# Attention steps joined for two units, six weight conversions moved from stage one to the slots, one Square moved from ScalarE to VectorE

## The chip, the cores and the metric

The kernel runs on one core of a Trainium2 chip. The metric is the time of one execution in microseconds (us), as the device measures it; lower is better. Beside it stands a profile of one execution, whose "span" runs from its first to its last recorded instruction. The engines are called PE (TensorE, the matrix unit), DVE (VectorE), ACT (ScalarE), POOL (GpSimd) and SP (SyncE, which here issues most of the DMAs, in the order in which they stand in its queue).

## The reference

```
def _attn_ref(q, k, v, g_norm):
    kv = np.einsum('bhsd,bhse->bhde', k, v)
    out = np.einsum('bhsd,bhde->bhse', q, kv)
    rms = np.sqrt(np.mean(out * out, axis=-1, keepdims=True) + 1e-06)
    return (out / rms * g_norm).astype(np.float32)
def _moe_ref(x, w_in, w_out):
    h = x @ w_in
    r = np.maximum(h, 0.0)
    g = r * r
    return (g @ w_out).astype(np.float32)
def _moe2_ref(x, w_in, w_out):
    h = x @ w_in
    g = h * np.cos(h)
    return (g @ w_out).astype(np.float32)
```

There are 8 batches of 8 heads, 576 positions and a head width of 64. The attention's output becomes a matrix x of 4608 tokens by 512, which goes through `_moe_ref` (512 to 2048 to 512) and then through `_moe2_ref` with other weights of the same shape. The weights come in float64 words, two 32-bit halves each.

## The kernel before

Every factor of a matmul that has to be exact is kept as a high and a low part (`xh` and `xl`, `wh` and `wl`, `gh` and `gl`), and a product is three matmuls: high by high, high by low, low by high. The name "conversion" below means the work on one piece of weights: a load of raw words into a buffer `raw`, then on DVE `e` (L119), `w` (L121, L124), `e` (L130), the value (L133) and sums of blocks (L177), on ACT a step on `e` (L120) between the first two and the high part `wh` (L189), on DVE the low part (L191), and then stores of both to DRAM (L193, L194), from which the matmuls' loads `wi` and `ws` fetch them later. The pool of `raw` has two buffers. The load of the conversion after next is issued (L148) once the stores of the earlier one in that buffer are through. `Stream.place` gives each conversion its position and cuts it into steps at small distances after that position.

**Stage one** is 72 chunks, counted by `n`: 9 tiles of 512 tokens by 8 blocks `f` of 128 columns of the first layer. A chunk is 12 matmuls of the first layer into one PSUM bank (`layer_in`, L385), the activation `act_relu2` (Relu, L394; Square, L395; high part `gh`, L396; all on ACT; low part `gl` on DVE, L397), and 12 matmuls of the second layer into four accumulators (`layer_out`, L419), two chunks later. In chunks up to `nAtt` = 49 the attention runs in between, in units: a pair of heads `p` of a batch `b`, by two halves `i`. Its banks are "o" and "ss"; from chunk 49 on all four banks `l0`, `l1`, `o`, `ss` serve the first layer. A unit goes through `att_a` (PE), `att_o` (ACT: `sq` L305, `og` L306, and for batches from `NEXACT` = 2 on also `sh` L312, then `sl` on DVE L313), `att_b` (PE sums of squares `ss`, ACT `r` L325 and `r2` L327), `att_c` (DVE, L335 to L337) and `att_e` (stores to DRAM, `x_d`). In the first two batches, called the head below, `att_d` also writes some pieces directly into `xh` and `xl`.

**The slots** follow: 30 of them, 10 for the first MoE's remaining blocks and 20 for the second MoE. In a slot seven products of blocks go into the banks FA and FB (`first_product`, L507), are combined on DVE and ACT (`h`, L531), and go through a second set of products into SA and SB (L606, L669). The loads `wi` (L481) for the products stand in SP's queue among the conversions' loads and stores.

Positions in the list `jobs` order the calls; a scheduler that knows the buffers then fixes the order on each engine. The list of conversions is placed by

```
        (pairs_in(0, range(NP, 2 * NP)) + pairs_in(1, range(3)), nAtt + 1, nA0 - 7),
        (pairs_in(1, range(3, 2 * NP)) + pairs_in(1, range(4, 6), "seven"), pos(1), pos(7)),
```

that is 14 conversions spread over chunks 50 to 65 and 14 over slots 1 to 7. `nA0` = 72 is the number of chunks and `pos(k)` the start of slot k.

Of the kernel before, what the change touches and what calls it, by code (L numbers as in the profile page):

```python
# [16 lines left out]
P = 128  # L17
# [5 lines left out]
def kernel(  # L23
# [278 lines left out]
    def att_o(o, *u):  # L302
        og = att_p.tile([P, HS], F32, tag="og", name="og", bufs=4)
        sq = att_p.tile([P, HS], F32, tag="sq", name="sq", bufs=3)
        nc.scalar.activation(out=sq, in_=o, func=AF.Square)  # L305
        nc.scalar.activation(out=og, in_=o, func=AF.Copy, scale=gcol)  # L306
        if u[0] < NEXACT:
            att[u] = (og, sq, None)
            return
        sh = att_p.tile([P, HS], F32R, tag="sh", name="sh", bufs=2)  # L310
        sl = att_p.tile([P, HS], F32R, tag="sl", name="sl", bufs=2)
        nc.scalar.copy(out=sh, in_=sq)  # L312
        nc.vector.tensor_tensor(out=sl, in0=sq, in1=as32(sh[:]), op=ALU.subtract)  # L313
        att[u] = (og, sh, sl)

    def att_b(*u):
        og, sh, sl = att[u]
        ss = bank("ss")[:, :HS]
        if u[0] < NEXACT:
            nc.tensor.matmul(ss, as32(ones[:]), sh[:], start=True, stop=True)  # L320
        else:
            nc.tensor.matmul(ss, ones[:], sh[:], start=True, stop=False)
            nc.tensor.matmul(ss, ones[:], sl[:], start=False, stop=True)
        r = att_p.tile([P, HS], F32, tag="r", name="r", bufs=2)
        nc.scalar.activation(out=r, in_=ss, func=AF.Abs_reciprocal_sqrt, scale=1.0 / D, bias=epsb)  # L325
        r2 = att_p.tile([P, HS], F32, tag="r2", name="r2", bufs=2)
        nc.scalar.activation(out=r2, in_=r, func=AF.Square)  # L327
        att[u] = (og, ss, r, r2)

    def att_c(*u):  # L330

        og, ss, r, r2 = att[u]
        m = att_p.tile([P, HS], F32, tag="m", name="m", bufs=2)
        xo = att_p.tile([P, HS], F32, tag="xo", name="xo", bufs=3)
        nc.vector.scalar_tensor_tensor(out=m, in0=ss, scalar=D * EPS, in1=r2, op0=ALU.add, op1=ALU.mult)  # L335
        nc.vector.scalar_tensor_tensor(out=m, in0=m, scalar=-3.0 * D, in1=r, op0=ALU.add, op1=ALU.mult)
        nc.vector.tensor_tensor(out=xo, in0=m, in1=og, op=ALU.mult)  # L337
        att[u] = xo

    def att_d(*u):  # L340
        b, p, hf = u
        xo = att[u]
        if b >= NEXACT:
# [622 lines left out]
```

## Time and profile before

| what | value |
|---|---|
| runs | 1589.66, 1588.98, 1587.4 us (median 1588.98) |
| the profiled execution's own time | 1588.0 us |
| its span | 1586.2 us |
| PE busy | 1552.5 us (98%) |
| DVE busy | 1243.9 us (78%) |
| ACT busy | 1073.7 us (68%) |
| HBM traffic over the span | 246 GB/s |

The time is some 1.8 us longer than the span. PE's busy time counts a matmul from its start to its modelled end, so two that follow each other overlap; whether PE runs at its pace in a stretch is seen better from the number of matmuls that start in it than from the busy share. [...]

### The profile page before, as it was taken

The page shows a single profiled execution, that of the slowest core. Times are in us where ns is not written, and L with a number is a line of the kernel's source. Part 1 is how long each engine was busy: PE and PEld are TensorE (multiplying, and loading weights), DVE is VectorE, ACT ScalarE, POOL GpSimd, SP SyncE. Part 2 cuts the span into 40 slices and gives each one's busy share as a digit, 9 for nine tenths or more (in the row PEclk, how much of TensorE's full clock was granted, in tenths as well). Part 3 has the DMA queues.
Part 4 walks back from the last instruction along what each step waited for, and adds up shares of the span by engine and source line. Part 5 has one row for each costly group of instructions (what it writes and reads, how often), then busy time and mean ns, then how long its engine had stood idle before and what let it go on. Part 6 is the DMA issues. An engine that isn't in the chain of part 4 may idle for free.

```text
span 1586.2 us, 24792 instructions
## 1 busy us (share of the span) xinstructions
PE 1552.5 (98%) x9164; PEld 1359.8 (86%) x9164; DVE 1243.9 (78%) x1688; ACT 1073.7 (68%) x1535; POOL 116.4 (7%) x125
## 2 busy tenths in 40 slices
PE   5999999999989999999999999999999999999998
PEld 4777777778777878888999899999999999999998
DVE  7977868798766798888747678967896788689677
ACT  5977768775545755555636667776777677777774
POOL 1100211111100000000000000000000001100110
PEclk9999999999999999999999999999999999999999
DMA  8855978777679989999987678988999889999995
GB/s 320 276 157 163 279 225 248 217 212 225 213 221 333 320 263 340 312 345 304 339 273 288 231 215 270 269 260 262 268 264 280 239 259 287 279 365 308 265 363 170
DMA packets 236951, 425.53 MB, mean 268 GB/s; under 512 B 18464, under 2 KB 155168, under 8 KB 236832
## 3 DMA queue, kind: packets, MB, share of 16 engines
q1 hardware_dynamic: 225840, 387.78, 72.9%
q0 software_dynamic: 10992, 36.18, 11.3%
q8 instruction: 73, 1.20, 0.3%
q14 instruction: 46, 0.38, 0.1%
HBM read 309.85 MB, written 80.22 MB: 246 GB/s over the span
## 4 chain that ended last, share of the span: by engine, by line
PE 83%; DVE 6%; DMA 5%; issue 3%; ACT 2%; SPq 0%; POOL 0%; DVEq 0%; ACTq 0%; POOLq 0%
PE FA L507 15%; PE FB L507 15%; PE SA L669 13%; PE SB L669 12%; PE acc L419 9%; PE l L385 9%; PE SB L606 3%; PE SA L606 3%; DMA wi_d<-raw 1%; DMA raw<-in_wB 1%; DMA sum<-part 1%; DMA q<-in_qT 1%; DVE raw L177 1%; ACT wh L189 1%; DMA raw<-in_wA 1%
## 5 line engine op out<-in xcount | busy, mean ns | idle before, releaser
L507 PE MATMUL FA<-xh,wi 128*128 128x512 f32 (+1 forms) x840 | 306.1, 370 | 1.1 <-ACT ev L405 0.9
L507 PE MATMUL FB<-xh,wi 128*128 128x512 f32 (+1 forms) x840 | 306.1, 370 | 0.0
L669 PE MATMUL SB<-ws,gh 128*128 128x256 f32 x1008 | 237.9, 280 | 1.1 <-ACT u L521 0.8
L669 PE MATMUL SA<-ws,gh 128*128 128x256 f32 x1008 | 237.9, 280 | 0.0
L669 PEld LDWEIGHTS SB<-ws,gh 128*128 128x128 f32 x1008 | 185.9, 188 | 14.4 <-ACT u L521 1.0
L669 PEld LDWEIGHTS SA<-ws,gh 128*128 128x128 f32 x1008 | 186.2, 188 | 13.2
L507 PEld LDWEIGHTS FA<-xh,wi 128*128 128x128 f32 x840 | 157.8, 188 | 11.0 <-ACT ev L405 1.3
L507 PEld LDWEIGHTS FB<-xh,wi 128*128 128x128 f32 x840 | 157.8, 188 | 8.2
L646 DVE TENSOR_TENSOR gl<-y,gh 128x1024 fp32r<-128x1024 f32 (+1 forms) x100 | 111.4, 1114 | 39.1 <-ACT gh L645 38.9
L669 PE MATMUL SA<-ws,gl 128*128 128x256 f32 x504 | 141.0, 280 | 1.1 <-DVE gl L646 1.1
L669 PE MATMUL SB<-ws,gl 128*128 128x256 f32 x504 | 141.2, 280 | 0.8 <-DVE gl L646 0.8
L695 POOL DMA_DIRECT2D sum<-part x71 | 60.3, 850 | 1100.8 <-ACT part L694 1082.2
L566 DVE SCALAR_TENSOR_TENSOR y<-y,h 128x1024 f32<-128x1024 f32 (+1 forms) x80 | 89.2, 1115 | 53.6 <-ACT y L562 53.2
L548 ACT ACTIVATE y<-h,zerob 128x1024 int32<-128x1024 f32 (+1 forms) x80 | 85.1, 1064 | 50.7 <-DVE h L527 50.7
L419 PE MATMUL acc<-gh,wh 128*128 128x512 f32 x288 | 114.5, 399 | 4.2 <-ACT gh L396 2.5
L419 PE MATMUL acc<-gl,wh 128*128 128x512 f32 x288 | 114.4, 397 | 2.1 <-DVE gl L397 2.1
L419 PE MATMUL acc<-gh,wl 128*128 128x512 f32 x288 | 113.6, 395 | 0.0
L507 PE MATMUL FA<-xl,wi 128*128 128x512 f32 (+1 forms) x300 | 111.0, 370 | 0.0
L507 PE MATMUL FB<-xl,wi 128*128 128x512 f32 (+1 forms) x300 | 110.9, 370 | 0.0
L669 PEld LDWEIGHTS SB<-ws,gl 128*128 128x128 f32 x504 | 94.7, 188 | 7.9 <-DVE gl L646 1.5
L669 PEld LDWEIGHTS SA<-ws,gl 128*128 128x128 f32 x504 | 94.7, 188 | 7.8 <-DVE gl L646 1.3
L645 ACT CAST gh<-y 128x1024 fp32r<-128x1024 f32 (+1 forms) x100 | 94.5, 957 | 6.1 <-DVE y L628 6.0
(178 smaller groups left out, 3781.6 us busy)
## 6 DMA issues: line engine op xcount, KB each, us to landing
wi<-wi_d SPq DMA_DIRECT2D x210, 512.0 KB, 6.9
ws<-ws_d SPq DMA_DIRECT2D x175, 512.0 KB, 5.8
sum<-part POOLq DMA_DIRECT2D x45, 512.0 KB, 7.7
kvld<-in_kv SPq DMA_DIRECT2D x32, 512.0 KB, 6.9
wi_d<-wh SPq DMA_DIRECT2D x24, 448.0 KB, 4.1
wi_d<-raw SPq DMA_DIRECT2D x24, 448.0 KB, 4.0
raw<-in_wA SPq DMA_DIRECT2D x20, 512.0 KB, 5.5
wo<-wo_d SPq DMA_DIRECT2D x20, 512.0 KB, 6.4
```

The source lines that it names most:

```text
L177: nc.vector.tensor_tensor(out=a[:, o], in0=a[:, x], in1=a[:, y], op=op)
L189: nc.scalar.copy(out=h, in_=a[:, lo:end])
L385: nc.tensor.matmul(ps, a[:, 0, cs], m[:], start=(c == 0 and k == 0), stop=(c == NKC - 1 and k == 2))
L419: nc.tensor.matmul(o, a[:, cs], m[:], start=(f == 0 and n == 0), stop=(f == NH - 1 and n == 2), skip_group_check=True)
L507: nc.tensor.matmul(ps[:, pp, :], a, b, start=(i in (0, 1, 2) and n == 0), stop=(n == 5), skip_group_check=True)
L548: nc.scalar.activation(out=y.bitcast(I32), in_=hs[k, b], func=AF.Identity, bias=zerob)
L566: nc.vector.scalar_tensor_tensor(out=y, in0=y, scalar=-2.0 * math.pi, in1=hs.pop((k, b)), op0=ALU.add, op1=ALU.mult)
L606: nc.tensor.matmul(ps, lhs, rhs, start=(a == 0 and (x, y) == (0, 0)), stop=last, skip_group_check=True)
L645: nc.scalar.copy(out=h, in_=src)
L646: nc.vector.tensor_tensor(out=l, in0=src, in1=as32(h), op=ALU.subtract)
L669: nc.tensor.matmul(ps[:, b, :], lhs, rhs, start=(i in (0, 1, 2) and n == 0 and (m == 0 or b % 2 == 0)), stop=(n == 5), skip_group_check=True,)
L695: nc.gpsimd.dma_start(out=e, in_=part, accum_op=ALU.add)
```

## The change

It has four parts. The attention's operations that touch SBUF alone (`sh`, `sl`, the second step of `att_c` and its product) are done once for the two units of a pair, on tiles of [128, 2, 288] in place of two of [128, 288]; the result takes the place of `m`, whose three buffers `sq` of the later batches shares; `r` and `r2` have one buffer in place of two; `x_d` is stored once both units are done. In the 23 chunks from 49 on, Square on ACT is replaced by one DVE operation that reads the PSUM bank and `r`. The steps of a conversion in the chunks after `nAtt` are spaced as before it. Six conversions (`pairs_in(1, range(3))`) move to the slots: 8 are spread over chunks 50 to 65, and 20 over slots 1 to 9.2.

```diff
@@ -299,52 +299,57 @@
         for i, o in enumerate(os):
             att_o(o, b, p, i)
 
-    def att_o(o, *u):
-        og = att_p.tile([P, HS], F32, tag="og", name="og", bufs=4)
-        sq = att_p.tile([P, HS], F32, tag="sq", name="sq", bufs=3)
-        nc.scalar.activation(out=sq, in_=o, func=AF.Square)
-        nc.scalar.activation(out=og, in_=o, func=AF.Copy, scale=gcol)
-        if u[0] < NEXACT:
-            att[u] = (og, sq, None)
+    def two(dtype, name, tag, bufs):
+        return att_p.tile([P, 2, HS], dtype, tag=tag, name=name, bufs=bufs)
+
+    def att_o(o, b, p, i):
+        if i == 0:
+            sq = two(F32, "sq", "sq", 2) if b < NEXACT else two(F32, "sq", "m", 3)
+            att[b, p] = {"og": two(F32, "og", "og", 2), "sq": sq}
+        a = att[b, p]
+        nc.scalar.activation(out=a["sq"][:, i], in_=o, func=AF.Square)
+        nc.scalar.activation(out=a["og"][:, i], in_=o, func=AF.Copy, scale=gcol)
+        if b >= NEXACT and i == 1:
+            sq = a["sq"]
+            a["sh"], a["sl"] = sh, sl = two(F32R, "sh", "sq", 2), two(F32R, "sl", "sl", 2)
+            nc.scalar.copy(out=sh, in_=sq)
+            nc.vector.tensor_tensor(out=sl, in0=sq, in1=as32(sh[:]), op=ALU.subtract)
+
+    def att_b(b, p, i):
+        a = att[b, p]
+        ss = a["ss", i] = bank("ss")[:, :HS]
+        if b < NEXACT:
+            nc.tensor.matmul(ss, as32(ones[:]), a["sq"][:, i], start=True, stop=True)
+        else:
+            nc.tensor.matmul(ss, ones[:], a["sh"][:, i], start=True, stop=False)
+            nc.tensor.matmul(ss, ones[:], a["sl"][:, i], start=False, stop=True)
+        if i == 0:
+            a["r"] = two(F32, "r", "r", 1)
+        r = a["r"][:, i]
+        nc.scalar.activation(out=r, in_=ss, func=AF.Abs_reciprocal_sqrt, scale=1.0 / D, bias=epsb)
+        r2 = a["r2", i] = att_p.tile([P, HS], F32, tag="r2", name="r2", bufs=1)
+        nc.scalar.activation(out=r2, in_=r, func=AF.Square)
+
+    def att_c(b, p, i):
+
+        a = att[b, p]
+        if i == 0:
+            a["m"] = two(F32, "m", "m", 3)
+        m = a["m"]
+        nc.vector.scalar_tensor_tensor(
+            out=m[:, i], in0=a["ss", i], scalar=D * EPS, in1=a["r2", i], op0=ALU.add, op1=ALU.mult
+        )
+        if i == 1:
+            nc.vector.scalar_tensor_tensor(out=m, in0=m, scalar=-3.0 * D, in1=a["r"], op0=ALU.add, op1=ALU.mult)
+            nc.vector.tensor_tensor(out=m, in0=m, in1=a["og"], op=ALU.mult)
+
+    def att_d(b, p, i):
+        if b >= NEXACT or i == 0:
             return
...
-    def att_d(*u):
-        b, p, hf = u
-        xo = att[u]
-        if b >= NEXACT:
-            return
-        tok = b * S + hf * HS
+        xo = att[b, p]["m"].rearrange("p i n -> p (i n)")
+        tok = b * S
         for t in range(NDIRECT):
-            lo, hi = max(tok, t * TOK), min(tok + HS, (t + 1) * TOK)
+            lo, hi = max(tok, t * TOK), min(tok + S, (t + 1) * TOK)
             if lo >= hi:
                 continue
             if (t, p) not in xs:
@@ -354,16 +359,18 @@
             nc.scalar.copy(out=h, in_=piece)
             nc.vector.tensor_tensor(out=l, in0=piece, in1=as32(h), op=ALU.subtract)
 
-    def att_e(*u):
-        b, p, i = u
-        xo = att.pop(u)
-        if b < NEXACT:
-            nc.gpsimd.dma_start(out=x_d[b][:, p, i * HS:(i + 1) * HS], in_=xo)
+    def att_e(b, p, i):
+        if i == 0:
             return
-        for hf in range(2):
-            nc.sync.dma_start(
-                out=x_d[b][i * D:(i + 1) * D, p, hf * HS:(hf + 1) * HS], in_=xo[hf * D:(hf + 1) * D]
-            )
+        xo = att.pop((b, p))["m"]
+        for i in range(2):
+            if b < NEXACT:
+                nc.gpsimd.dma_start(out=x_d[b][:, p, i * HS:(i + 1) * HS], in_=xo[:, i])
+                continue
+            for hf in range(2):
+                nc.sync.dma_start(
+                    out=x_d[b][i * D:(i + 1) * D, p, hf * HS:(hf + 1) * HS], in_=xo[hf * D:(hf + 1) * D, i]
+                )
 
     def att_units(b):
         return [(b, p, i) for p in range(NKC) for i in range(2)]
@@ -387,12 +394,15 @@
                     )
         return pss
 
-    def act_relu2(ps):
+    def act_relu2(ps, busy):
         r, g = (temp([P, TOK], F32, n) for n in "rg")
         h = g_p.tile([P, TOK], F32R, tag="gh", name="gh")
         l = g_p.tile([P, TOK], F32R, tag="gl", name="gl")
         nc.scalar.activation(out=r, in_=ps, func=AF.Relu)
-        nc.scalar.activation(out=g, in_=r, func=AF.Square)
+        if busy:
+            nc.scalar.activation(out=g, in_=r, func=AF.Square)
+        else:
+            nc.vector.scalar_tensor_tensor(out=g, in0=ps, scalar=0.0, in1=r, op0=ALU.max, op1=ALU.mult)
         nc.scalar.copy(out=h, in_=g)
         nc.vector.tensor_tensor(out=l, in0=g, in1=as32(h[:]), op=ALU.subtract)
         return h, l
@@ -730,7 +740,7 @@
             for k, (n, item) in enumerate(zip(positions, self.items)):
                 steps = (0, 0.06, 0.13, 0.3, 0.45)
                 if n < nA0:
-                    steps = (0, 0.25, 0.5, 0.75, 1.0, 1.25, 1.4) if n < nAtt else (0, 0.15, 0.3, 0.5, 1.0)
+                    steps = (0, 0.25, 0.5, 0.75, 1.0, 1.25, 1.4)
                 if self.use != conv_w or item[0] == "one":
                     at(n, self.use, *item)
                     steps = (after,)
@@ -752,8 +762,8 @@
         w_at += [n + step * k for k in range(len(new))]
     for new, n0, n1 in (
         (pairs_in(0, range(4, 6), "seven") + outs_of(0, range(6, 8)) + pairs_in(1, range(6, 8), "seven") + pairs_in(1, range(4), "seven"), 13, nAtt + 1),
-        (pairs_in(0, range(NP, 2 * NP)) + pairs_in(1, range(3)), nAtt + 1, nA0 - 7),
-        (pairs_in(1, range(3, 2 * NP)) + pairs_in(1, range(4, 6), "seven"), pos(1), pos(7)),
+        (pairs_in(0, range(NP, 2 * NP)), nAtt + 1, nA0 - 7),
+        (pairs_in(1, range(2 * NP)) + pairs_in(1, range(4, 6), "seven"), pos(1), pos(9.2)),
     ):
         w_items += new
         w_at += [n0 + (n1 - n0) / len(new) * k for k in range(len(new))]
@@ -834,7 +844,7 @@
                 ps = first[n]
             else:
                 ps, = layer_in(*chunks[n])
-            gs[chunks[n]] = act_relu2(ps)
+            gs[chunks[n]] = act_relu2(ps, n < nAtt)
             run_jobs(n)
             if n >= LAG:
                 layer_out(*chunks[n - LAG])
```

On ACT's queue, where the weight conversions of the last chunks of stage one stand (`g` is Square, L395; `gh` L396; `e` and `wh` belong to conversions), this was before:

```order
L394 ACTIVATE r<-l_4922 128x512
L395 ACTIVATE g<-r 128x512
L396 CAST gh<-g 128x512
L189 CAST wh<-raw 128x896
L238 CAST xh<-xraw 128x512 x3
L394 ACTIVATE r<-o 128x512
L120 ACTIVATE e<-e,expb 128x512
L395 ACTIVATE g<-r 128x512
L396 CAST gh<-g 128x512
L189 CAST wh<-raw 128x896
```

and this stands there after the change, at the same chunks:

```order
L401 ACTIVATE r<-l_4520 128x512
L406 CAST gh<-g 128x512
L120 ACTIVATE e<-e,expb 128x512
L238 CAST xh<-xraw 128x512 x3
L401 ACTIVATE r<-o 128x512
L189 CAST wh<-raw 128x896
L406 CAST gh<-g 128x512
L401 ACTIVATE r<-ss 128x512
L406 CAST gh<-g 128x512
L120 ACTIVATE e<-e,expb 128x512
```

The Square is gone from ACT, and a step of a conversion stands before about every second `gh` where one or two stood before each.

On DVE's queue, this stood before in slot 7, between two of its additions `h` out of the banks FA and FB (`sum` adds the second set's results, `xt` and `xl` prepare the next tile's factors):

```order
L531 TENSOR_TENSOR h<-FA,m_7959 128x2x384
L628 TENSOR_TENSOR t<-h,t 128x2x384
L457 TENSOR_TENSOR xt<-xraw 128x2x384
...
L697 TENSOR_TENSOR sum<-SB,sum 128x2x384
L457 TENSOR_TENSOR xt<-xraw,xt 128x2x384
L646 TENSOR_TENSOR gl<-h,gh 128x2x384
L457 TENSOR_TENSOR xraw<-xraw 128x2x384
L697 TENSOR_TENSOR sum<-SA,sum 128x2x384
L531 TENSOR_TENSOR h<-FB,m_8101 128x2x384
```

and this stands there after the change:

```order
L707 TENSOR_TENSOR sum<-SB,sum 128x2x384
L119 TENSOR_SCALAR e<-raw 128x512
L121 TENSOR_SCALAR w<-raw 128x512
L656 TENSOR_TENSOR gl<-h,gh 128x2x384
L124 SCALAR_TENSOR_TENSOR w<-raw,w 128x512
L130 SCALAR_TENSOR_TENSOR e<-raw,e 128x512
L467 TENSOR_TENSOR xt<-xraw,xt 128x2x384
L133 SCALAR_TENSOR_TENSOR raw<-w,e 128x512
L467 TENSOR_TENSOR xraw<-xraw 128x2x384
L177 TENSOR_TENSOR raw<-raw 128x128 x3
L486 TENSOR_TENSOR xl<-xt,xh 128x2x384
L541 TENSOR_TENSOR h<-FB,m_7656 128x2x384
```

A conversion (L119 to L177) now lies ahead of the second addition.

In the attention's stretch, ACT's queue held this for the two units of a pair of a later batch:

```order
L305 ACTIVATE sq<-l_2547 128x288
L306 ACTIVATE og<-l_2547,gcol 128x288
L312 CAST sh<-sq 128x288
L305 ACTIVATE sq<-o 128x288
L306 ACTIVATE og<-o,gcol 128x288
```

and holds this now, with one `sh` for both further on:

```order
L310 ACTIVATE sq<-l_2338 128x288
L311 ACTIVATE og<-l_2338,gcol 128x288
L310 ACTIVATE sq<-o 128x288
L311 ACTIVATE og<-o,gcol 128x288
```

The first unit's `sh` no longer comes ahead of the second unit's `sq`.

## Rows read from the trace of the kernel before

**Rows 1.** PE's waits, us 80 to 360: total, times, longest.

```profile
PE o L298 <- ACT kvx L277: 0.5, 1, 0.5
```

**Rows 2.** Stretches: each engine's busy us (count); then PEclk, DMA share, GB/s.

```profile
400.00:420.00 20.00, 18.89 (x83) 15.06 (x81) 15.01 (x27) 9.59 (x17) 4.56 (x3) 1.00 0.64 191
420.00:440.00 20.00, 19.44 (x85) 15.90 (x86) 16.28 (x34) 11.05 (x18) 0.00 (x0) 1.00 0.74 236
440.00:460.00 20.00, 19.68 (x87) 15.96 (x86) 15.35 (x33) 9.92 (x15) 0.00 (x0) 1.00 0.66 199
460.00:480.00 20.00, 15.73 (x56) 11.73 (x56) 13.92 (x28) 11.23 (x18) 0.00 (x0) 0.83 0.95 292
480.00:500.00 20.00, 20.00 (x90) 16.57 (x89) 12.40 (x17) 10.17 (x17) 0.00 (x0) 1.00 0.99 356
```

**Rows 3.** Waits of the engines, us 364 to 480: total, times, longest.

```profile
DVE e L119 <- DMA raw<-in_wB: 8.2, 5, 3.6
...
PE acc L419 <- ACT gh L396: 2.5, 1, 2.5
PE acc L419 <- DVE gl L397: 2.1, 3, 1.4
...
PE acc L419 <- DVE ev L407: 1.7, 1, 1.7
```

**Rows 4.** Timelines of DVE, ACT and PE: start us, us, engine, line.

```profile
462.90 0.43 DVE L119 TENSOR_SCALAR e<-raw 128x512 uint32<-128x512 uint32 x1 [2.30 <-DMA raw<-in_wB]
464.97 0.62 ACT L396 CAST gh<-g 128x512 fp32r<-128x512 f32 x1
465.64 0.50 PE L419 MATMUL acc<-gh,wh 128*128 128x512 f32 x1 [2.48 <-ACT gh L396]
```

**Rows 5.** Waits of SP's queue, us 364 to 480, the largest.

```profile
SPq L148 <- DMA wi_d<-raw: 36.0, 13, 4.1
```

**Rows 6.** One conversion on DVE, timeline, its first and last row.

```profile
454.13 0.43 DVE L119 TENSOR_SCALAR e<-raw 128x512 uint32<-128x512 uint32 x1
...
459.50 1.09 DVE L191 TENSOR_TENSOR raw<-raw,wh 128x896 fp32r<-128x896 f32 x1 [1.02 <-ACT wh L189]
```

**Rows 7.** DMA issues: count, KB each, median us to landing.

```profile
wi_d<-raw SPq DMA_DIRECT2D x24, 448.0 KB, 4.0
...
raw<-in_wB SPq DMA_DIRECT2D x32, 256.0 KB, 3.5
```

**Rows 8.** DVE by line: ns min/median/max; L335 reads PSUM, L336 SBUF.

```profile
L335 DVE SCALAR_TENSOR_TENSOR m<-ss,r x58: 443/452/459, 23.8 to 359.6; 128x288 f32<-128x288 f32 x58
L336 DVE SCALAR_TENSOR_TENSOR m<-m,r x64: 445/454/1581, 24.9 to 360.6; 128x288 f32<-128x288 f32 x64
```

**Rows 9.** Stretches in slots 7 and 8, columns as in rows 2.

```profile
757.00:819.00 62.00, 62.00 (x350) 60.78 (x349) 38.95 (x43) 31.43 (x41) 0.00 (x0) 1.00 0.85 295
768.00:790.00 22.00, 22.00 (x129) 22.00 (x128) 21.85 (x25) 17.61 (x23) 0.00 (x0) 1.00 1.00 388
```

**Rows 10.** Waits of SP's queue, us 640 to 860, the largest.

```profile
SPq L193 <- ACT wh L189: 25.7, 7, 6.8
```

**Rows 11.** A `wi` load of slot 7: issue, landing (seven such), first use.

```profile
769.46 0.64 SPq L481 DMA_DIRECT2D wi<-wi_d  x1
DMA to landing us min/median/max: 4.9/7.2/9.7
783.58 0.33 PE L507 MATMUL FB<-xh,wi 128*128 128x384 f32 x1
```

**Rows 12.** PE's waits of us 18.5 to 65 on ACT, the largest.

```profile
PE ss L320 <- ACT sq L305: 2.0, 1, 2.0
...
PE acc L320 <- ACT sq L305: 1.5, 1, 1.5
```

**Rows 13.** ACT's Relu, us 80 to 360: busy, mean ns, idle before.

```profile
L394 ACT ACTIVATE r<-l 128x512 f32<-128x512 f32 x42 | 25.2, 599 | 34.5 <-PE l L385 33.9 <-issue 0.4
```

**Rows 14.** Stores `x_d`, from issue to landing.

```profile
DMA to landing us min/median/max: 1.9/3.1/8.7
```

More of the change, by code (lines that the diff above doesn't have):

```diff
@@ L300, in att_a @@
             att_o(o, b, p, i)
-    def att_o(o, *u):
-        og = att_p.tile([P, HS], F32, tag="og", name="og", bufs=4)
-        sq = att_p.tile([P, HS], F32, tag="sq", name="sq", bufs=3)
-        nc.scalar.activation(out=sq, in_=o, func=AF.Square)
-        nc.scalar.activation(out=og, in_=o, func=AF.Copy, scale=gcol)
-        if u[0] < NEXACT:
-            att[u] = (og, sq, None)
-            return
[L310 to L338, printed above, removed]
-    def att_d(*u):
-        b, p, hf = u
-        xo = att[u]
-        if b >= NEXACT:
-            return
-        tok = b * S + hf * HS
+    def two(dtype, name, tag, bufs):
+        return att_p.tile([P, 2, HS], dtype, tag=tag, name=name, bufs=bufs)
```

## The prediction

> **What bounds the kernel now.** I read the page first: PE is busy 98% of the span, DVE 78%, ACT 68%. So only a stretch in which PE misses matmuls can give time back, and I looked next for those stretches, in PE's own waits. In the attention's stretch there is next to nothing: 0.5 us between 80 and 360 us [rows 1]. At the end of stage one there is something. A clean stretch of 20 us there starts 90 matmuls, one per 0.222 us; the four stretches from 400 to 480 us start 83, 85, 87 and 56 [rows 2]. That is 311 where 360 fit, so 49 are missing, and 49 x 0.222 = 10.9 us are lost. [...]
>
> Who made PE wait? PE's waits on `gh`, `gl` and `ev` come to 2.5 + 2.1 + 1.7 = 6.3 us, and in the same stretch DVE's first step of a conversion waits 8.2 us for its raw words [rows 3]. The timelines tie the two together: DVE's `e` starts at 462.90 after 2.30 us of waiting for `raw`, ACT's `gh` comes behind the conversion's step on ACT, at 464.97, and PE's second layer starts at 465.64, 2.48 us late [rows 4]. ACT and DVE work in order, so a conversion whose words are late holds the activation behind it. The words are late because SP waits, 36.0 us in 13 times, for a buffer `raw` whose stores are still under way [rows 5].
>
> **The change part by part.** *Six conversions leave the end of stage one.* A buffer is held from its load (3.5 us) through the work on DVE and ACT, 454.13 to 460.59 or 6.5 us [rows 6], to the end of its store, 4.0 us [rows 7]: 14.0 us, and with two buffers one conversion per 7.0 us. A chunk takes 24 x 0.222 = 5.33 us. 14 conversions over 15 chunks come every 1.07 chunks or 5.7 us, faster than the buffers turn round; 8 over 15 come every 1.88 chunks or 10.0 us, slower. [...] The bounds are 0 and 10.9 us; I take 10.0, nearly all, since a wait or two at the tile boundaries (`ev`) may stay. The other spacing of the steps makes the load that follows later by 0.4 chunks, 2.1 us; 10.0 - 7.0 = 3.0 us of room covers it. Without that room it would cost as much as now.
>
> *Square moves from ACT to DVE, 23 times.* DVE loses 6 x 4.8 us of conversions (6.46 us less the 1.02 us of waiting and some 0.6 us of a `gl` in between [rows 6]), 29 us, and gains 23 operations on 512 columns. A conversion's own operation of that size and form bounds one from above: its last, on 896 columns, takes 1.09 us [rows 6]; from below, 288 columns take 0.45 us [rows 8]. In between lies 0.7 us, or 16 us in all. DVE was busy 15.4 of 20 us there [rows 2], so it has room, and the activation has two chunks, 10.7 us, until PE wants it. I count this at nothing; what hides it is that lag of two chunks, and if a conversion on DVE waited for its words again, `g` would now wait behind it as `gl` does.
>
> The new operation reads PSUM, and that could be dearer: the trace gives 452 ns for the step that reads PSUM and 454 ns for the same step on SBUF alone [rows 8], so I take no surcharge. [...]
>
> *The six go to the slots.* 20 over 8.2 slots are one per 0.41 slots, where 14 over 6 were one per 0.43. So slots 1 to 6 change little, and some five conversions fall into slots 7 and 8, 757 to 819 us, that had none. DVE there is busy 38.95 of 62 us [rows 9]; five times 4.8 us makes 63. The transfers moved 295 GB/s x 62 us = 18.3 MB [rows 9]; five conversions add, each, two loads of 256 KB, a store of 448 KB of the low part [rows 7] and as much of the high part, 1408 KB or 1.44 MB, 7.2 MB in all. 25.5 MB at the highest rate held over a long stretch, 388 GB/s [rows 9], take 65.7 us: the transfers end up 3.7 us late, DVE about 1 us. And SP's queue waits for conversions' high parts, 25.7 us in 7 times, 6.8 us at the longest [rows 10], with loads `wi` behind. What covers it: a `wi` is issued at 769.46, lands 7.2 us later in the median, and is first used at 783.58, 6.9 us after that [rows 11]. The mean wait on SP (3.7 us) with the late transfers and DVE makes 3.7 + 3.7 + 1.0 = 8.4 us against 6.9 of cover, 1.5 us lost; the longest (6.8) makes 11.5, 4.6 us lost, and that once in each of the two slots 9.2 us. From below the loss is nothing. I take 2 us, near the mean case.
>
> *The joins.* In the later batches they shorten DVE and ACT, but PE there waits 0.5 us in all [rows 1]: nothing. In the head PE does wait for ACT, 2.0 and 1.5 us [rows 12]; joined steps free some of it, up to 3.5 us, but a joined step also waits for the second unit, 0.45 us [rows 8] in each of 8 pairs, 3.6 us at the worst. I take a gain of 0.5 us, with 3.5 us either way.
>
> **The sum.** 1588.0 (the profiled execution) - 10.0 + 0 + 2.0 - 0.5 = 1579.5 us. The median of the runs lies 1.0 us above the profiled one, so the forecast is 1580.5 us. 0.2%, about what a measurement of this kernel can tell from no change, is 3.2 us.
>
> **The rivals.** *The slots give it back.* DVE near 100% and transfers at their limit in slots 7 to 9 cost the worst of above, 9.2 us: 1589.0 - 10.0 + 9.2 - 0.5 = 1587.7 us, no change. For it speaks that 768 to 790 us is full already on DVE (21.85 of 22) and at a DMA share of 1.00 [rows 9]; against it the lighter rest of slot 8. [...]
>
> *Slower: ACT stalls on the shared buffers.* `sq` of the later batches now takes a buffer that earlier held a finished `m`, and so waits for four stores of three pairs ago. A pair starts every 1.75 chunks, three take 5.25, and `att_e` of a pair's second unit comes 0.875 + 2.5 = 3.4 chunks after the pair's start; that leaves 1.9 chunks of 280 / 42 = 6.7 us, 12.5 us, for stores that land in 3.1 us, 8.7 at most [rows 14]. Behind `sq` on ACT stand `og` and the next Relu, for which PE waits. ACT stood idle 33.9 us before 42 Relus, 0.8 us each [rows 13], 1.4 us per pair of 1.75 chunks. Of 24 pairs about 11 get such a buffer; the change is slower by over 0.2% when these lose (8.5 + 3.2) / 11 = 1.1 us each, so from a stall of 2.5 us, and at 4 us the loss is 29 us: 1580.5 + 29 = 1609 us. The single buffers of `r` and `r2` could stall in the same place; DVE reads them right after ACT writes them, and ACT has the same 1.4 us.
>
> *It doesn't do what it says:* the words still come late for eight conversions, because the loads wait in SP's queue for something else than `raw`. Half the gain is left: 1585.5 us.
>
> *All covers hold:* the slots cost nothing and the head gives its 3.5 us: 1589.0 - 10.0 - 3.5 = 1575.5 us.
>
> **Chances.** The forecast (1577 to 1584) 0.58; all covers hold 0.08; half the gain 0.11; slots give it back 0.14; ACT stalls 0.09. Faster by over 0.2% (under 1585.8): 0.58 + 0.08 + two thirds of 0.11 and some 0.03 of the slots' case = 0.76; slower (above 1592.2): 0.08; between: 0.16. The range runs from 1575 to 1588, which leaves out the stalls and little else.
>
> **What would show it.** Right: from 400 to 480 us near 90 matmuls per 20 us, a granted clock of 1.00, no wait of DVE's `e` on `raw` there; conversions up to some 810 us, and DVE near 95% in slots 7 and 8 with PE's waits on `wi` or FA and FB under 3 us. Wrong: waits of ACT's `sq` on `x_d` between 80 and 360 us, of SP on `raw` from 400 on, or of PE on `wi` after 760 us.

## The result, and the profile after

The changed kernel takes 1599.78 us in the median (1596.22 to 1601.72, 6 runs), the kernel before 1588.19 us (1585.21 to 1589.7, 6 runs). The ratio is 1.0074, with a 95% interval of 1.0063 to 1.0085: 11.6 us slower, where 8 us faster was forecast. The profiled execution took 1600.09 us.

The lines of the changed kernel lie 6 to 13 below those of before (Relu is L401, Square on DVE L405, `gh` L406, `gl` L407, the products L517 and L679). First the stretches at the end of stage one, which answer to [rows 2], with the same columns:

```profile
400.00:420.00 20.00, 20.00 (x90) 16.57 (x89) 17.05 (x28) 10.43 (x18) 4.30 (x3) 1.00 0.38 114
420.00:440.00 20.00, 20.00 (x90) 16.58 (x89) 15.23 (x30) 7.32 (x12) 0.00 (x0) 1.00 0.79 241
440.00:460.00 20.00, 20.00 (x90) 16.57 (x89) 16.16 (x30) 9.02 (x13) 0.00 (x0) 1.00 0.76 232
460.00:480.00 20.00, 20.00 (x89) 16.55 (x89) 13.60 (x17) 8.06 (x12) 0.00 (x0) 1.00 0.61 203
```

359 matmuls start where 311 did, and PEclk, the granted clock of TensorE as a share of its full speed, stays at 1.00, where before the last of them had 0.83. VectorE's waits there, which answer to [rows 3], us 364 to 480:

```profile
DVE g L405 <- ACT r L401: 18.4, 12, 3.4
...
DVE g L405 <- DMA raw<-in_wA: 0.5, 1, 0.5
DVE e L119 <- DMA raw<-in_wA: 0.4, 1, 0.4
```

The waits for raw words are gone, as forecast. The time is lost elsewhere. PE does the same matmuls in both kernels, in nearly the same order in stage one and in the same order in the slots, so the start of one and the same matmul in both timelines shows how far the changed kernel is ahead or behind:

| the first matmul of | before, us | after, us | behind by | change |
|---|---|---|---|---|
| chunk 13 | 127.1 | 132.9 | 5.8 | +5.8 (the head) |
| chunk 49 | 364.8 | 370.8 | 6.0 | +0.2 |
| slot 0 | 507.1 | 502.5 | -4.6 | -10.6 (the end of stage one) |
| slot 0's sixth product | 521.0 | 520.0 | -1.0 | +3.6 (the passage) |
| slot 7 | 756.6 | 755.1 | -1.5 | -0.5 |
| slot 8 | 787.7 | 788.8 | 1.1 | +2.6 |
| slot 9 | 818.5 | 820.9 | 2.3 | +1.2 |
| slot 10 | 848.2 | 860.0 | 11.8 | +9.5 |
| (the last matmul) | 1581.2 | 1593.2 | 12.0 | +0.2 |

So 10.6 us are won at the end of stage one; 5.8 us are lost in the head, 3.6 us in the passage into the slots, and 13.3 us in slots 7 to 9. The sum, 12.0 us, is the difference of the two profiled executions (1600.09 and 1588.0 us, 12.1).

Slots 7 to 9, after; the first row answers to [rows 9]:

```profile
757.00:819.00 62.00, 59.17 (x330) 56.93 (x329) 55.93 (x83) 33.98 (x45) 0.00 (x0) 1.00 0.99 329
760.00:860.00 100.00, 90.23 (x498) 87.48 (x498) 84.47 (x112) 56.11 (x72) 0.00 (x0) 0.98 1.01 356
```

and the second of these stretches in the kernel before:

```profile
760.00:860.00 100.00, 100.00 (x562) 97.79 (x561) 73.55 (x79) 56.03 (x69) 0.00 (x0) 1.00 0.88 309
```

VectorE is not full (84 of 100 us), but the DMA engines are: a share of 1.01 for 100 us, at 356 GB/s. What PE waits for in us 740 to 870 are nearly all results of VectorE and ScalarE, and only 0.2 us are put down to a load (`wo`):

```profile
PE SA L679 <- issue: 4.7, 1, 4.7
PE SB L679 <- DVE sum L707: 1.7, 1, 1.7
PE FA L517 <- ACT m L531: 1.7, 1, 1.7
PE SA L679 <- ACT xh L485: 1.5, 2, 1.0
PE SB L616 <- DVE sum L629: 0.3, 1, 0.3
PE SA L616 <- DMA wo<-wo_d: 0.2, 1, 0.2
```

The longest wait has no releaser that the profile names ("issue"), but the timelines show one. The matmul that ends it, at 842.18, writes the bank SA anew, and VectorE's `sum`, which reads SA, ends at 842.08. The product that this `sum` adds had been ready for 8.5 us when it started (its last matmul ends at 832.66), but on VectorE the `sum` stood behind other operations, of which `gl` waited 2.68 us for ScalarE. VectorE's rows and the matmul:

```profile
839.12 0.96 DVE L656 TENSOR_TENSOR gl<-h,gh 128x768 fp32r<-128x768 f32 x1 [2.68 <-ACT gh L655]
839.99 1.22 DVE L467 TENSOR_TENSOR xt<-xraw 128x1024 f32<-128x1024 f32 x1
841.13 0.95 DVE L707 TENSOR_TENSOR sum<-SA,sum 128x768 f32<-128x768 f32 x1
...
842.18 0.41 PE L679 MATMUL SA<-gh,ws 128*128 128x384 f32 x1 [4.66 <-issue]
```

In the kernel before, the same `sum` starts as soon as its product is done (the last matmul ends at 830.32):

```profile
830.35 0.96 DVE L697 TENSOR_TENSOR sum<-SA,sum 128x768 f32<-128x768 f32 x1 [0.16 <-PE SA L669]
```

The loads of weights came in time. Of the loads `wi` and `ws` for slots 7 to 9 none landed after its first use. The closest is the `wi` load of [rows 11]: issued at 777.48, landed 4.9 us later, first used at 783.61, 1.3 us after it had landed.

In the attention's stretch, us 9 to 360, ScalarE has a wait that before has not (it has none for VectorE's step on `m`):

```profile
ACT r L329 <- DVE m L343: 9.4, 9, 1.6
```

That is the next pair's `r`, waiting for the last reader of the single buffer.

### The profile page after: what moved, and what is told of

Its sections match the earlier page's. It is cut to its first block, busy times and chain, and to the rows that moved or that the text cites. A ratio compares the mean times of both kernels' runs of the same rounds, so it can differ in the third digit from the quotient of the medians.

```text
span 1598.2 us, 24647 instructions
## 1 busy us (share of the span) xinstructions
PE 1553.9 (97%) x9164; PEld 1361.0 (85%) x9164; DVE 1250.9 (78%) x1615; ACT 1058.9 (66%) x1480; POOL 117.0 (7%) x125
## 4 chain that ended last, share of the span: by engine, by line
PE 82%; DVE 6%; DMA 6%; ACT 3%; issue 2%; SPq 1%; POOL 0%; DVEq 0%; ACTq 0%; POOLq 0%
PE FA L517 14%; PE FB L517 14%; PE SA L679 12%; PE SB L679 11%; PE acc L429 11%; PE l L392 10%; PE SB L616 2%; PE SA L616 2%; DMA wi<-wi_d 2%; PE o L392 1%; PE ss L392 1%; DVE sum L707 1%; PE o L264 1%; DMA raw<-in_wB 1%; DMA q<-in_qT 1%
## 5 line engine op out<-in xcount | busy, mean ns | idle before, releaser
L517 PE MATMUL FA<-xh,wi 128*128 128x512 f32 (+1 forms) x840 | 306.0, 372 | 4.9 <-ACT m L531 3.5
L517 PE MATMUL FB<-xh,wi 128*128 128x512 f32 (+1 forms) x840 | 305.5, 371 | 0.0
L679 PE MATMUL SB<-ws,gh 128*128 128x256 f32 x1008 | 237.9, 280 | 0.9 <-ACT u L531 0.5
L679 PE MATMUL SA<-ws,gh 128*128 128x256 f32 x1008 | 237.9, 280 | 0.0
L679 PEld LDWEIGHTS SB<-ws,gh 128*128 128x128 f32 x1008 | 186.0, 188 | 14.2 <-ACT u L531 0.7
L679 PEld LDWEIGHTS SA<-ws,gh 128*128 128x128 f32 x1008 | 186.2, 188 | 13.1
L517 PEld LDWEIGHTS FA<-xh,wi 128*128 128x128 f32 x840 | 158.1, 188 | 15.6 <-ACT m L531 4.5
L517 PEld LDWEIGHTS FB<-xh,wi 128*128 128x128 f32 x840 | 158.5, 189 | 8.2
L679 PE MATMUL SA<-ws,gl 128*128 128x256 f32 x504 | 141.0, 280 | 1.1 <-DVE gl L656 1.1
L679 PE MATMUL SB<-ws,gl 128*128 128x256 f32 x504 | 141.2, 280 | 0.8 <-DVE gl L656 0.7
L517 PE MATMUL FA<-xl,wi 128*128 128x512 f32 (+1 forms) x300 | 111.5, 372 | 0.0
L517 PE MATMUL FB<-xl,wi 128*128 128x512 f32 (+1 forms) x300 | 111.4, 371 | 0.0
L679 PEld LDWEIGHTS SB<-ws,gl 128*128 128x128 f32 x504 | 94.7, 188 | 7.9 <-DVE gl L656 1.5
L679 PEld LDWEIGHTS SA<-ws,gl 128*128 128x128 f32 x504 | 94.7, 188 | 7.8 <-DVE gl L656 1.3
L392 PE MATMUL l<-xh,wh 128*128 128x512 f32 x240 | 96.7, 403 | 4.1 <-ACT xh L359 3.1
```

Of the source, the lines that this page charges most:

```text
L392: nc.tensor.matmul(ps, a[:, 0, cs], m[:], start=(c == 0 and k == 0), stop=(c == NKC - 1 and k == 2))
L517: nc.tensor.matmul(ps[:, pp, :], a, b, start=(i in (0, 1, 2) and n == 0), stop=(n == 5), skip_group_check=True)
L679: nc.tensor.matmul(ps[:, b, :], lhs, rhs, start=(i in (0, 1, 2) and n == 0 and (m == 0 or b % 2 == 0)), stop=(n == 5), skip_group_check=True,)
```

## The experiments

Each run's ratio is to the kernel before on the same chip, with its 95% interval. "Behind" is read as in the table above: how far a matmul starts behind its twin in the kernel before, in the profiled execution. Both belong together, since the profiled execution can lie some us from the median: the run on the joins was 8.3 us behind in its profile and 12.6 us in its median.

| run | ratio (interval) | behind at chunk 13 | chunk 49 | slot 0 | slot 7 | slot 10 | end |
|---|---|---|---|---|---|---|---|
| the change | 1.0074 (1.0063 to 1.0085) | 5.8 | 6.0 | -4.6 | -1.5 | 11.8 | 12.0 |
| e1_conversions | 1.0035 (1.0022 to 1.0047) | -0.2 | 0.1 | -10.6 | -8.8 | 6.7 | 5.9 |
| e2_joins | 1.008 (1.0067 to 1.0093) | 4.2 | 4.8 | 8.3 | 8.2 | 8.2 | 8.3 |
| e3_square | 1.0024 (1.0014 to 1.0034) | -0.8 | -0.7 | 4.3 | 4.6 | 4.6 | 4.4 |
| e4_single_r | 1.0024 (1.001 to 1.0038) | 4.0 | 4.5 | 5.4 | 5.9 | 5.8 | 5.3 |
| e5_joins_late | 1.0049 (1.0035 to 1.0063) | 4.5 | 11.9 | 12.9 | 12.9 | 12.9 | 13.0 |
| e6_stores_pool | 1.0173 (1.0159 to 1.0187) | 5.8 | 10.5 | 0.0 | 19.2 | 28.3 | 26.9 |
| e7_dve_light | 1.0092 (1.0079 to 1.0105) | 5.3 | 8.3 | -2.2 | 0.4 | 15.5 | 14.9 |
| e8_no_stores | 1.0005 (0.9996 to 1.0013) | 5.0 | 8.6 | -1.9 | 1.0 | 2.5 | 1.9 |
| e9_spread | 0.9978 (0.997 to 0.9987) | -0.4 | 0.1 | -10.6 | -7.1 | -4.0 | -5.0 |
| e10_spread_square | 0.9983 (0.9973 to 0.9994) | -0.4 | 0.2 | -10.4 | -7.1 | -3.9 | -3.2 |
| e11_ten | 0.9985 (0.9974 to 0.9997) | -0.6 | -0.3 | -11.0 | -7.7 | 0.9 | 0.6 |
| e12_after_spread | 1.004 (1.0025 to 1.0056) | 5.8 | 9.1 | -1.5 | 4.9 | 8.1 | 8.7 |
| e13_joins_two_r | 1.0096 (1.0083 to 1.0109) | 10.4 | 14.8 | 16.4 | 15.8 | 15.8 | 16.0 |
| e14_four_kv | 1.0084 (1.0067 to 1.0101) | 8.2 | 14.6 | 15.0 | 14.8 | 14.8 | 15.5 |

**The parts, one by one.** Three kernels take one part of the change alone. The move (with the new spacing of the steps) on the kernel before (e1_conversions):

```diff
-                    steps = (0, 0.25, 0.5, 0.75, 1.0, 1.25, 1.4) if n < nAtt else (0, 0.15, 0.3, 0.5, 1.0)
+                    steps = (0, 0.25, 0.5, 0.75, 1.0, 1.25, 1.4)
...
-        (pairs_in(0, range(NP, 2 * NP)) + pairs_in(1, range(3)), nAtt + 1, nA0 - 7),
-        (pairs_in(1, range(3, 2 * NP)) + pairs_in(1, range(4, 6), "seven"), pos(1), pos(7)),
+        (pairs_in(0, range(NP, 2 * NP)), nAtt + 1, nA0 - 7),
+        (pairs_in(1, range(2 * NP)) + pairs_in(1, range(4, 6), "seven"), pos(1), pos(9.2)),
```

> The kernel before with the move of the six conversions and the new spacing of their steps alone. Theory A (the changed kernel's loss sits in three places that the parts own one by one: the joins the head, the move the slots): the head as before, the end of stage one gains 8 to 10.5 us, the passage to slot 0 gives 3 to 4 us back, slots 7 to 9 lose 11 to 14 us; together 4 to 9 us slower than before, ratio 1.0025 to 1.0055, and from 820 to 860 us over 6 us of PE's time are missing. Theory B (the parts lose together only, because the joins and the Square put conversions into another order on the engines): the slots lose less than 5 us and the kernel is 3 to 6 us faster than before, ratio under 0.998.

It was 4.6 us slower in the median, as theory A had it. The move owns the whole gain of stage one (10.7 us from chunk 49 to slot 0) and gives 15.5 us back between slots 7 and 10, somewhat more than the 11 to 14 expected; the passage costs 1.9 us, less than the 3 to 4 expected. The gain of the end of stage one owes nothing to the Square or to the joins. PE stops before the same matmul for the same 4.66 us, and again just after the end of `sum` out of SA:

```profile
836.02 0.95 DVE L697 TENSOR_TENSOR sum<-SA,sum 128x768 f32<-128x768 f32 x1
...
837.07 0.41 PE L669 MATMUL SA<-gh,ws 128*128 128x384 f32 x1 [4.66 <-issue]
```

The joins alone (the diff's hunks on `att_o` to `att_e`) (e2_joins):

> The kernel before with the attention's joins alone (and their buffers: one for r and r2, m shared with sq). Theory A: the head (up to 140 us) loses 4 to 6 us, nothing between 140 and 860 us changes by more than 1.5 us; 3.5 to 7 us slower, ratio 1.002 to 1.0045. Theory B: the head's loss in the changed kernel comes from the order of jobs that the other parts shift, and the joins alone are within 2 us of before.

The place was right in part: 4.2 us are lost in the head, but 3.5 us more between chunk 49 and slot 0, where theory A had under 1.5. The size was under-estimated: 1.008, 12.6 us in the median. What the joins lose behind the head isn't explained by any run.

The Square alone (the diff's hunks on `act_relu2`) (e3_square):

> The kernel before with Square moved from ScalarE to VectorE in 23 chunks alone. If the waits at the end of stage one go because conversions are fewer (the prediction's step): they stay here, with DVE's waits on raw of 6 to 11 us, and the time is within 2 us of before, ratio 0.9985 to 1.0015. Rival: ScalarE's queue was what held the activation, and the Square's departure alone frees it: over 5 us of the 10.9 us come back and the kernel is 5 us or more faster, ratio under 0.997.

Neither: 4.1 us slower, and all of it between chunk 49 and slot 0. With 14 conversions there VectorE still waits for raw words, and now `g` stands behind them, and the bank that it reads stays taken. Its waits, us 364 to 505:

```profile
ACT gh L399 <- DVE g L398: 16.5, 18, 1.9
...
DVE e L119 <- DMA raw<-in_wB: 6.1, 4, 3.3
...
PE l L385 <- DVE g L398: 3.4, 1, 3.4
```

The three parts alone add up to 21 us, all together cost 11.6. For the Square the reason is shown below: beside the move, which takes away the waits behind which it stands, it costs nothing (e10_spread_square). That part of what the joins lose later goes the same way is not shown.

**Slots 7 to 9: which resource?** On the changed kernel, the last six conversions without VectorE's work (e7_dve_light). These weights are not computed, and other weights are used in their place:

```diff
-            w, e = words(raw, [P, 4, P])
+            n = 1 if (kind, m, f, i) in LIGHT else P
+            w, e = words(raw, [P, 4, P], n)
...
-                nc.vector.tensor_tensor(out=a[:, o], in0=a[:, x], in1=a[:, y], op=op)
+                nc.vector.tensor_tensor(out=a[:, o, :n], in0=a[:, x, :n], in1=a[:, y, :n], op=op)
...
```

> The changed kernel, with VectorE's work of the last six conversions (those of slots 6.7 to 8.8) cut to one column of 128, so those weights are not computed; their raw words come from another tensor and the matmuls load other weights in their place, with loads, stores and ScalarE's steps of the same sizes. Theory D (VectorE is full, and what it does late comes late everywhere): of the 15 us missing from 760 to 860 us at least 9 come back, ratio 0.999 to 1.003. Theory E (the transfers): 10 us or more stay missing, ratio over 1.005.

And the same six with all of their work, but without their stores (e8_no_stores):

```diff
-                nc.sync.dma_start(out=dst[:, lo - 1:end - 1, 0, :], in_=as32(h))
-            nc.sync.dma_start(out=dst[:, :, 1, :], in_=as32(l[:, 1:]))
+                if (kind, m, f, i) not in LIGHT:
+                    nc.sync.dma_start(out=dst[:, lo - 1:end - 1, 0, :], in_=as32(h))
+            if (kind, m, f, i) not in LIGHT:
+                nc.sync.dma_start(out=dst[:, :, 1, :], in_=as32(l[:, 1:]))
...
```

> The changed kernel without the stores of the last six conversions (0.92 MB each, 5.5 MB), the matmuls that would load them load others of the same size. Theory E (the transfers are at their limit): the 15 us missing from 760 to 860 us fall to under 6, ratio 0.999 to 1.004. Theory C the same, since no store stands in SyncE's queue, so this run tells E and C from D together with the run that moves the stores. Theory D: 10 us or more stay missing, ratio over 1.005.

Us 760 to 860 of the first and of the second, columns as above:

```profile
760.00:860.00 100.00, 89.25 (x485) 86.94 (x484) 67.97 (x111) 52.92 (x70) 0.00 (x0) 0.97 1.01 356
```

```profile
760.00:860.00 100.00, 99.10 (x554) 96.25 (x553) 90.98 (x120) 61.24 (x77) 0.00 (x0) 1.00 0.91 337
```

With VectorE's busy time down from 84 to 68 us PE still starts only 485 matmuls, where the changed kernel starts 498, and the transfers still run at 356 GB/s and a share of 1.01. With 5.5 MB of stores less the share is 0.91, VectorE is at 91 us, and PE starts 554 of 562: from slot 7 to slot 10 only 1.5 us are lost in place of 13.3. So theory D falls: the amount of VectorE's work is not the cause, and without the stores the loss is gone.

That the transfers are the cause, as theory E has it, is not shown by this, for two reasons. Without the stores the order of the instructions on VectorE is another one as well: there `sum` out of SA follows `xt` directly and starts as soon as its product is done, as in the kernel before, and PE's stop of 4.66 us is gone, while the run with VectorE's light work still has the changed kernel's order and the same stop of 4.66 us. And full DMA engines alone do not make the loss: e9_spread, below, has them as full over the same 100 us (a share of 1.00, at 357 GB/s) and loses 3.1 us between slot 7 and slot 10:

```profile
760.00:860.00 100.00, 97.91 (x545) 94.46 (x545) 91.28 (x124) 63.16 (x79) 0.00 (x0) 1.00 1.00 357
```

The transfers may still stand behind the stop. `xt`, just ahead of the late `sum`, reads a load `xraw` that landed at 838.9, in the kernel before at 831.3. No run changes the transfers and keeps the order, or the reverse.

E and C (SyncE's queue) both fit the storeless run. The changed kernel with the stores of these conversions on GpSimd's queue was to part them (e6_stores_pool):

```diff
-                nc.sync.dma_start(out=dst[:, lo - 1:end - 1, 0, :], in_=as32(h))
-            nc.sync.dma_start(out=dst[:, :, 1, :], in_=as32(l[:, 1:]))
+                store = nc.gpsimd if where else nc.sync
+                store.dma_start(out=dst[:, lo - 1:end - 1, 0, :], in_=as32(h))
+            store.dma_start(out=dst[:, :, 1, :], in_=as32(l[:, 1:]))
```

> The changed kernel, with the stores of the conversions in the slots issued on GpSimd's queue in place of SyncE's. Theory C (SyncE's queue: stores that wait for ScalarE and VectorE hold the weight loads behind them): of the 15 us that PE misses from 760 to 860 us at least 8 come back, and the kernel is 2 to 5 us slower than before (ratio 1.001 to 1.003) in place of 11.6. Theories D (VectorE is full there) and E (the transfers are at their limit): 10 us or more stay missing there, ratio over 1.005.

It was 26 us slower than before, and it moved more than intended: the eight conversions at the end of stage one went to that queue too. It lost 19 us between slot 0 and slot 7, where the changed kernel loses 3. In slots 0 to 7, fifteen stores `wi_d<-raw` in either kernel, those on GpSimd's queue took longer to land, and SyncE, which waits for them before it loads the next raw words, waited twice as long. The rows are of the changed kernel (us 502 to 755), then of this run (us 507 to 776):

```profile
wi_d<-raw SPq DMA_DIRECT2D x15, 448.0 KB, 5.5
...
SPq L148 <- DMA wi_d<-raw: 32.4, 14, 3.8
```

```profile
wi_d<-raw POOLq DMA_DIRECT2D x15, 448.0 KB, 7.5
...
SPq L148 <- DMA wi_d<-raw: 66.4, 12, 9.6
```

For the four stores `ws_d<-raw` of slots 7 to 9 there was no such difference: 8.7 us on SyncE's queue, 8.2 us on GpSimd's.

So getting the stores out of SyncE's queue is no cure. Between slot 7 and slot 10 this run lost 9.1 us in place of 13.3, which neither theory had, so it does not part C from E. SyncE's waits speak against theory C as it was worded: in us 740 to 870 of the changed kernel the longest for VectorE or ScalarE is 2.2 us, while the storeless run, which loses next to nothing, has one of 10.0 us (us 740 to 860). Whether the loss comes from late transfers, from SyncE's queue or from the order on the engines stays open.

**A version without that density.** The move alone, with the 20 conversions spread over more slots (they are used from slot 10 on, the last ones in slot 13), e9_spread; the edit is shown against e1_conversions:

```diff
-        (pairs_in(1, range(2 * NP)) + pairs_in(1, range(4, 6), "seven"), pos(1), pos(9.2)),
+        (pairs_in(1, range(2 * NP)) + pairs_in(1, range(4, 6), "seven"), pos(1), pos(12)),
```

> The kernel before with the move of the six conversions and the spacing of their steps, without joins and without the moved Square, and with the 20 conversions spread over slots 1 to 12 in place of 1 to 9.2, so 1.8 per slot in place of 2.4. If the price of the move is the density of conversions in slots 7 to 9: the end of stage one keeps its 8 to 9 us, the slots lose under 6 in place of 15, and the kernel is 2 to 7 us faster than before, ratio 0.9955 to 0.9985. If slots 7 to 9 can carry none at all: still 10 us or more lost there, ratio over 1.0.

1584.9 us, 0.9978 (0.997 to 0.9987): faster than both kernels, and the fastest here together with the next two runs, whose ratios lie within its interval. Between slot 0 and slot 10 it loses 6.6 us, 2.0 of them in the passage, where the move with the denser slots (e1_conversions) loses 17.3. The same with the Square (e10_spread_square):

> The run on the spread (slots 1 to 12, no joins) with Square moved to VectorE in the 23 chunks as well. If the Square costs 4 us alone only because a conversion on VectorE waits for its words, it costs nothing here: within 1.5 us of the run on the spread, ratio to before 0.9965 to 0.999. If it is dear in itself (a longer way from the bank to gh), it costs 3 to 5 us here too: ratio 1.0 to 1.002.

The difference to the run before it is within both intervals, though the profiled executions differ by 1.8 us at the end: where no conversion waits for its words, the moved Square costs nothing, and brings nothing. With ten conversions in stage one (`pairs_in(1, range(1))` stays there), e11_ten:

> The run on the spread with ten conversions left at the end of stage one in place of eight (one per 8.0 us) and 18 in place of 20 over slots 1 to 12. By the buffers' cycle of 7.0 us ten still fit: no wait of VectorE on raw over 1 us from 400 to 500 us, the end of stage one keeps 8 us or more of its gain, and the slots lose 1 to 3 us less than with 20; ratio to before 0.9945 to 0.9975. If the cycle is longer than 8 us, 2 us or more of the waits come back there.

Half right. Ten fit, with 0.2 us of waits on raw in all, but slots 7 to 9 lose more, not less (8.6 us between slot 7 and slot 10, against 3.1), and the ratio of 0.9985 misses its range. This run has fewer conversions per slot than e9_spread, so their density is not the whole of it; why was not followed up. And the whole changed kernel with the wider spread (e12_after_spread):

> The whole changed kernel with its 20 conversions over slots 1 to 12 in place of 1 to 9.2. If the density in slots 7 to 9 is what the move costs there: of the 15 us missing from 760 to 860 us 8 to 12 come back, and what stays over before is the head's 5 us and the passage to slot 0: ratio 0.9985 to 1.0035.

From slot 7 to slot 10 it loses 3.2 us in place of 13.3, as expected. The total, 1.004, is worse than its range by a little: at chunk 49 the run was 9.1 us behind, where the changed kernel was 6.0, and from slot 0 to slot 7 it lost 6.4 us, where the changed kernel lost 3.1. Stage one has the same source in this run, in the changed kernel and in the runs with the light or storeless conversions, and they were 6.0 to 9.1 us behind at chunk 49. The order of the instructions on ScalarE and VectorE is not wholly the same in them, so whether this spread belongs to the execution is not shown.

**The joins.** Joined in the later batches only, with the same buffers (e5_joins_late):

> The joins alone as in the run on the joins, but the first two batches take the second step, the product, the direct pieces and the stores by single units again; the buffers are those of the joins (one pair tile r, one r2). If the head loses because a joined step waits for its second unit: the loss of the joins goes, within 1.5 us of before. If it loses because the next pair's r waits for the single buffer: at least half of the joins' loss stays, 2 to 5 us slower than before, ratio 1.001 to 1.003.

1.0049, above its range, and 4.5 us behind at chunk 13: the head loses as much without a joined step in it. What waits for a second unit is not the cause there. From chunk 13 to 49 it lost 7.4 us, where the joins alone lost 0.6; that is not explained, and its profiled execution is 5.3 us above its median. Then nothing joined, but the buffers (e4_single_r):

```diff
-        r = att_p.tile([P, HS], F32, tag="r", name="r", bufs=2)
+        if u[2] == 0:
+            att["r"] = att_p.tile([P, 2, HS], F32, tag="r", name="r", bufs=1)
+        r = att["r"][:, u[2]]
...
-        r2 = att_p.tile([P, HS], F32, tag="r2", name="r2", bufs=2)
+        r2 = att_p.tile([P, HS], F32, tag="r2", name="r2", bufs=1)
```

> The kernel before with nothing joined, only r as one tile for a pair of units with one buffer and r2 with one buffer, as the changed kernel has them. Theory F (the joins lose through these single buffers: ScalarE's next r waits for VectorE's last reader, PE's next ss behind it): at least half of the joins' loss is here, 4 to 12 us slower than before, ratio 1.0025 to 1.0075, with ScalarE's waits for VectorE's step on m and PE's waits of ss for it before 360 us. Theory G (the joined steps themselves are what comes late, or m's shared buffers): within 2 us of before, ratio 0.9987 to 1.0013.

4.4 us in the median and 4.0 us behind at chunk 13, with the wait in ScalarE, us 9 to 360:

```profile
ACT r L327 <- DVE m L338: 3.4, 4, 1.3
```

That is the head's loss almost whole, and a third of the joins' median of 12.6. Theory F's "at least half" is met in the profiled executions (5.3 of 8.3 us) and missed in the medians. The last pair of runs gave both buffers back, and took the room from the loads of k and v (`KVB = 4`); first the joins (e13_joins_two_r), then the control (e14_four_kv):

> The joins alone with two buffers each for r and r2, the room taken from the attention's loads of k and v (four buffers in place of five). Theory F (the single buffers are what the joins lose by): ScalarE's waits of r for VectorE's step on m before 360 us, 9.5 us in 9 times with one buffer, fall under 2 us, and the time is within 2.5 us of its control, the kernel before with four kv buffers. Theory G (the joined steps come late for both units): 5 us or more over the control.

> The kernel before with four buffers for the loads of k and v in place of five, a control for the run on the joins with two buffers: within 3 us of before, ratio 0.999 to 1.002.

The control missed: one kv buffer less costs 13.5 us by itself, and PE's waits for these loads are 9.1 us longer (the rows are of the control, then of the kernel before):

```profile
PE o L264 <- DMA kvld<-in_kv: 20.1, 6, 9.3
```

```profile
PE o L264 <- DMA kvld<-in_kv: 11.0, 4, 9.2
```

Against that control the joins with two buffers are 2.1 us slower, and ScalarE's `r` waits for VectorE no more. This speaks for theory F, but next to a wait of 20 us a smaller one can hide, so the share of the joined steps themselves in the later batches stays open.

## Why the prediction was wrong, step by step

- **The end of stage one** (10.0 us of gain): right in place, mechanism and size, 10.6 us. The estimate of 7.0 us for the buffers' cycle fits eight conversions and ten (0.9 and 0.2 us of VectorE's waits for raw words).
- **The Square at nothing:** right beside the move (the two spread runs, which have no joins, agree within their intervals), and the condition put on it was right too: where conversions wait, it costs 4.1 us.
- **The six in the slots** (2.0 us): the term that failed most, 13.3 us. The step that failed is the wait. The working let late transfers reach PE through a `wi` load that comes later than its cover of 6.9 us allows [rows 11]. That cover did shrink, to 1.3 us, but no load of these slots came after its first use. PE stopped for results of VectorE and ScalarE instead, at the longest 4.66 us for the `sum` out of SA, which stood behind other work on VectorE. And the working ended at 819 us, while 9.5 of the 13.3 us fell in slot 9, where the kernel before already ran at a full DMA share:

```profile
818.50:848.20 29.70, 29.70 (x174) 29.70 (x173) 26.28 (x28) 20.29 (x25) 0.00 (x0) 1.00 1.00 369
```

That the slots would be full of transfers was right, and that the move is what costs time there is shown (e1_conversions; e8_no_stores and e12_after_spread take the loss away). How it leads to VectorE's late `sum`, by the transfers, by SyncE's queue or by another order on the engines, stays open. VectorE's "63 of 62 us" played no part: it measured 55.93, and taking its work away gave nothing back (e7_dve_light).

- **The transfers' rate** (388 GB/s, on the strength of a stretch of 22 us) was neither held nor a bound: over 100 us the mean was 356 and, in the spread run, 357 GB/s, but 40 us ran at 398 and 20 us at 413 GB/s; and the spread run loses only 3.1 us at its 357 GB/s.
- **The joins** (a gain of 0.5 us): wrong in sign, a loss of 5.8 us in the head. The rival about the single buffers had the mechanism, but the sentence that set it aside, that VectorE reads `r` right after ScalarE writes it, failed: VectorE's last reader came late enough that ScalarE waited 9.4 us in 9 times, 4.3 us of it before us 133. The single buffers alone, with nothing joined, lost 4.0 us by chunk 13 (e4_single_r). The other half of that rival, `sq` waiting for stores of `x_d`, did not come: no such wait shows.
- **The passage to slot 0** (3.6 us) was in no term. PE comes to slot 0 10.6 us sooner than its place behind the head would give, and the first factors of the slots wait for buffers that the last stores of stage one still hold, as ScalarE's timeline shows:

```profile
508.06 1.04 ACT L485 CAST xh<-xraw 128x1024 fp32r<-128x1024 f32 x1 [6.63 <-DMA p_d<-ev]
```

The wait ends 5.6 us after slot 0's first matmul. The kernel before has the same wait, of 4.53 us, and there it ends 3.6 us after that matmul. But with the move and no joins the passage costs only 1.9 to 2.0 us (e1_conversions, e9_spread), though PE comes as much sooner, so coming sooner is at most a part. It was not tried by an experiment.

## What to carry to other kernels

Work that is moved out of a stretch where PE waits must be priced at the place where it arrives, over all of the stretch that it reaches, the part that is already full included. The slack of the loads is not enough for that price: here the loads came in time, and PE stopped for a result that VectorE had behind other work, so what the other engines have to do ahead of PE's results has to be looked at too. Count a ring of buffers when operations are joined: one buffer less for `r` and for `r2` cost 4.4 us, where the joins were to give 0.5. And a part that costs time alone can be free beside another that removes the wait behind which it stands, so parts should be run both alone and together.

## What the runs showed of the hardware

The rate of the DMA engines at a full share was not one number: 356 GB/s over us 760 to 860, and in the same execution 398 GB/s over us 820 to 860 and 413 GB/s over us 840 to 860. The packets differ with it: three quarters of them are under 2 KB in the first of these stretches and half of them in the last. No run changed the packets alone.

```profile
820.00:860.00 40.00, 33.06 (x180) 32.16 (x179) 29.82 (x32) 21.23 (x27) 0.00 (x0) 0.96 1.04 398
840.00:860.00 20.00, 15.55 (x78) 14.97 (x79) 18.54 (x20) 9.55 (x13) 0.00 (x0) 0.91 1.04 413
```

```profile
DMA packets 22896, 35.59 MB, mean 356 GB/s; under 512 B 1429, under 2 KB 17139, under 8 KB 22889
DMA packets 3208, 8.27 MB, mean 413 GB/s; under 512 B 281, under 2 KB 1584, under 8 KB 3207
```

The clock had its part: over us 840 to 860, in which PE starts again after the wait of 4.66 us, the granted clock was 0.91 on average, and from us 843 to 845.9 it was 0.50. In that stretch matmuls of 384 columns started every 0.32 us, in us 846 to 848, at 0.99, every 0.17 us, so by these numbers some 1.3 us of those 2.9 were lost on top of the wait (an estimate). The kernel before has such a stretch after PE's wait of 2.48 us at the end of stage one: 0.50 in us 468 to 472, where matmuls of 512 columns started every 0.43 us, against 0.23 us at 1.00. That the wait brings the low clock is not shown. Two of the us at 0.50 in the changed kernel:

```profile
844.00:846.00 2.00, 2.00 (x8) 2.00 (x7) 2.00 (x3) 0.48 (x1) 0.00 (x0) 0.50 1.05 407
```
